# Attention scores on 64x128 tiles, with the scale moved from the turned queries into the maximum pass

## Chip, core and metric

The kernel runs on one core of one Trainium2 chip. The metric is the device time of one execution in microseconds. In the profile the engines are PE (TensorE matmul), PEld (its weight loads), DVE (VectorE), ACT (ScalarE), POOL (GpSimd) and SP (SyncE, whose queue issues nearly all DMAs).

## What is computed

```python
def _attn_ref(q, k, v, tau):            # 8 batches, 8 heads, 576 rows, 64 columns
    scale = 1.0 / np.sqrt(q.shape[-1])
    scores = scale * np.matmul(q, k.transpose(0, 1, 3, 2))
    thresh = np.max(scores, axis=-1, keepdims=True) - tau
    scores = np.where(scores >= thresh, scores, -1000000000.0)
    scores = scores - np.max(scores, axis=-1, keepdims=True)
    attn = np.exp(scores)
    attn = attn / (np.sum(attn, axis=-1, keepdims=True) + 1e-09)
    return np.matmul(attn, v)

def _moe_ref(x, w_in, w_out):           # 4608x512, 512x2048, 2048x512
    h = np.maximum(x @ w_in, 0.0)
    return h * h @ w_out
```

The attention output, with its heads side by side, is `x`. All of it is float32; the two weight matrices arrive as float64 and are converted on the core.

## The kernel before

**Stages.** First comes attention, in 72 periods (`period`, L631). Periods 2 to 34 also convert the weights (`CONVERTING`, the names c1 to c6: L208, L214, L221, L229, L237, L248); periods 35 to 71 don't (`PLAIN`), and POOL adds up weight blocks there. Then come the two dense layers, done as sums and products of blocks (L946 and L1085 on PE, L125 and L128 on DVE and POOL). The change touches attention alone.

**Units.** Two heads of a batch are a pair; there are 32 pairs. The 576 query rows of a pair are four blocks of 128 and a rest of 64. A *unit* is one block of one pair, for both of its heads (j = 0, 1); the rests of two pairs form one unit together. So two pairs give 4 + 4 + 1 units, 144 in all, 16 of them shared by two pairs. A period computes the scores and the softmax of two units, called A and B, and the value products of the two units of two periods before.

**The steps of a period.** The lists `PLAIN` and `CONVERTING` (L606 and L609) write out the order by hand; each engine runs its part of a list in this order.

- *T*, `turn` (L399): PE transposes rows of q or of k, 64 rows at a time (L406), on tiles of 64 rows by 128 columns, into two banks of PSUM. *eT* copies the result to SBUF. For q that is two scaled copies of 256 columns on ACT (L413, an activation with `scale=qscale`, a column of 128 values, each -1/8). For k it is two plain copies (L421, 256 and 320 columns), and a scaled one (L413, 64 columns) for the query rest, whose rows are turned along with the keys. Every pair has a turn of q and a turn of k, so nine periods have four of each, and one has none.
- *SA*, *SB*, `scores` (L434): products of queries and keys. The contraction is over 64 values (one head), so the PE array is used in tiles. Before, all are tiles of 64x64: per unit two heads times two halves of 64 query rows, each a matmul of 512 columns (the first eight 64-key blocks) and one of 64 (the rest). SA does the 512 columns of A, and then the 64 of A and of B; SB does the 512 of B. A float32 matmul shows as two records.
- *topA0* and so on, `top` (L463): for each unit and head DVE reads 576 columns of scores from PSUM, multiplies them by a constant 1.0, writes them to SBUF, and takes the minimum (the scale is negative, so the minimum stands for the maximum). The accumulator is read by a second record. These four are "the passes" below. PLAIN has them as A1, A0, B1, B0.
- *least* (L470, POOL) adds tau to the minimum. *pow* (L473, ACT) is the exponential. *mask* (L478, DVE) sets what is below the threshold to zero, and sums; its threshold is a column of 128 values.
- *over*, *inv* (L485 POOL, L488 DVE): the reciprocals of the sums. *spread* (L528, POOL) widens them to 64 columns each.
- *U*, *V*, *W* (`half_turn`, L388): PE transposes the weights, also on 64x128 tiles; W also turns the widened reciprocals. *eU*, *eV*, *eW* (L535) are the copies on ACT.
- *PV*, `values` (L544): products of values and turned weights, on 64x64 tiles, into banks 0 and 5.
- *x* (L658 to L671): the two heads' products leave PSUM. Head 0's is multiplied by the reciprocals on DVE as it is read (L665, 128 columns); head 1's is copied by ACT (L667). *xs* (L682): POOL multiplies head 1's copy by its reciprocals. Then DMAs store x.

**What shares banks.** Scores, turned rows, the turn W and value products share six banks of PSUM. Unit A's scores lie in banks 0, 1, 4 and 5, unit B's in 1 to 4, the value products in 0 and 5, turned rows in 1 and 4, W in 2 and 3. `touch` (L363) adds a wait wherever two engines meet in a bank: PV waits for the passes over A, SA waits for the copies of x, the rest columns wait for eT, SB waits for eW. U and V use two further banks and wait for each other's copies.

In PLAIN the order on PE is SA, SB, V, PV, T, W, U; in CONVERTING it is T, SA, U, SB, PV, V, W.

## Time and profile before

| | |
|---|---|
| Median of three runs | 1281.25 us (1281.09 to 1282.95) |
| Span of the profiled execution, first to last instruction | 1278.6 us |
| Median less that span | 2.65 us |
| First pass (L463) of the first and of the last period | 9.5 us and 479.5 us |
| PE busy over the span | 1255.2 us (98%) |
| DVE, ACT, POOL busy over the span | 1000.2, 855.6, 897.4 us (78%, 67%, 70%) |
| Granted TensorE clock | 1.000 |

The shares over the whole span mix attention, in which PE, DVE and ACT are all busy nearly throughout, with the dense layers, in which PE alone is. What bounds attention has to be read from its own stages. A timeline row has the start (us from the span's start), the time until the last of its records ends, the engine, the line, the operation, the tiles written and read, the shape, the count, and in brackets the idle time before it with what ended that. Records on ACT and PE overlap: the next one can start before the last has ended, so what one of them costs is the distance between starts. A windows row has, for each engine, its busy time and its records in brackets.

### The profile page before, as it was taken

What the parts mean: (1) busy time and instruction counts of PE and PEld (TensorE: products, weight loads), DVE (VectorE), ACT (ScalarE), POOL (GpSimd) and SP (SyncE); (2) the same over time, 40 slices, a digit from 0 to 9 for tenths busy, and PEclk for the clock granted to TensorE, in tenths of its full rate; (3) what the DMA queues carried; (4) which work ended last, traced back from release to release, by engine and by line L of the source; (5) the groups of instructions that cost most, each with busy time, mean ns of one, the idle gap of its engine ahead of it and who ended that gap; (6) DMA issues with size and microseconds to landing.
All of it is one profiled execution on the core that took longest, in us unless ns stands there. A gap on an engine that the chain in (4) does not pass through costs nothing.

```text
span 1278.6 us, 44201 instructions
## 1 busy us (share of the span) xinstructions
PE 1255.2 (98%) x17459; PEld 1087.0 (85%) x17459; DVE 1000.2 (78%) x2449; ACT 855.6 (67%) x1552; POOL 897.4 (70%) x1094
## 2 busy tenths in 40 slices
PE   8999999999999999999999999999999999999998
PEld 6666666677777768988888888999999999999998
DVE  6999999999999997787878877877645664565463
ACT  6999999999999995666765767667422441343240
POOL 2565665655555557888798889858877777786775
PEclk9999999999999999999999999999999999999999
DMA  6566666544333413457666666589635414522511
GB/s 155 152 158 160 165 193 182 151 94 112 89 83 84 97 34 98 156 164 219 198 190 204 192 198 187 177 324 394 208 122 166 133 50 149 166 95 76 161 35 34
DMA packets 256591, 191.89 MB, mean 150 GB/s; under 512 B 96000, under 2 KB 217344, under 8 KB 256384
## 3 DMA queue, kind: packets, MB, share of 16 engines
q1 hardware_dynamic: 254928, 188.63, 49.8%
q8 instruction: 137, 2.24, 0.7%
q14 instruction: 70, 0.57, 0.1%
q10 hardware_dynamic: 1456, 0.44, 0.1%
HBM read 116.65 MB, written 72.35 MB: 148 GB/s over the span
## 4 chain that ended last, share of the span: by engine, by line
PE 70%; DMA 1%; ACT 1%; DVE 1%; issue 1%; ACTq 0%; DVEq 0%; SPq 0%
PE po L1085 30%; PE ph L946 27%; PE sc L544 5%; PE sc L445 4%; PE pt L388 2%; DMA wall<-w 1%; PE sc L406 1%; PE sc L388 1%; DVE arena L128 1%; DVE arena L463 0%; DMA g<-arena 0%; ACT arena L916 0%; ACT c L879 0%; DMA arena<-xT 0%; ACT arena L917 0%
## 5 line engine op out<-in xcount | busy, mean ns | idle before, releaser
L128 POOL TENSOR_TENSOR arena<-arena 128x512 f32<-128x512 f32 (+1 forms) x314 | 377.7, 1222 | 126.3 <-DVE arena L128 89.4
L1085 PE MATMUL po<-wall,arena 128*128 128x128 f32 x3528 | 394.4, 275 | 0.2 <-DVE arena L125 0.2
L1085 PEld LDWEIGHTS po<-wall,arena 128*128 128x128 f32 x3528 | 394.1, 192 | 0.4 <-DVE arena L125 0.4
L946 PE MATMUL ph<-arena,wall 128*128 128x128 f32 (+1 forms) x2352 | 387.4, 327 | 1.1 <-DVE arena L665 0.5
L946 PEld LDWEIGHTS ph<-arena,wall 128*128 128x128 f32 x2352 | 354.2, 191 | 34.2 <-DVE arena L128 2.2
L128 DVE TENSOR_TENSOR arena<-ph,arena 128x512 f32<-128x512 f32 x378 | 255.6, 688 | 75.8 <-PE ph L946 50.0
L125 POOL TENSOR_TENSOR arena<-arena 128x128 f32<-128x128 f32 (+2 forms) x314 | 255.2, 814 | 29.1 <-DMA arena<-w 10.7
L879 ACT COPY c<-arena 128x512 f32<-128x512 f32 (+2 forms) x319 | 176.1, 558 | 104.2 <-DVE arena L125 85.7
L473 ACT ACTIVATE arena<-arena 128x576 f32<-128x576 f32 x288 | 232.1, 918 | 16.7 <-DVE arena L463 16.7
L128 DVE TENSOR_TENSOR arena<-po,arena 128x128 f32<-128x128 f32 x378 | 108.3, 290 | 168.0 <-PE po L1085 167.4
L478 DVE SCALAR_TENSOR_TENSOR arena<-arena 128x576 f32<-128x576 f32 x288 | 225.5, 811 | 0.4 <-POOL arena L470 0.4
L463 DVE TENSOR_SCALAR_CACHE_REDUCE arena<-sc 128x576 f32<-128x576 f32 x288 | 204.5, 751 | 14.3 <-ACT arena L535 6.4
L125 DVE TENSOR_TENSOR arena<-arena,c 128x512 f32<-128x512 f32 (+2 forms) x283 | 176.8, 633 | 7.9 <-ACT c L879 6.1
L544 PEld LDWEIGHTS sc<-arena 64*64 64x64 f32 x5760 | 144.4, 133 | 43.1 <-DVE arena L463 39.1
L445 PE MATMUL sc<-arena 64*64 64x64 f32 (+1 forms) x2304 | 170.0, 415 | 0.3 <-DVE arena L665 0.3
L544 PE MATMUL sc<-arena 64*64 64x128 f32 (+1 forms) x5760 | 160.8, 262 | 8.5 <-DVE arena L463 5.8
L535 ACT COPY arena<-pt 128x1024 f32<-128x1024 f32 x144 | 166.0, 1153 | 1.6 <-PE pt L388 1.5
L769 ACT COPY arena<-po 128x128 f32<-128x128 f32 x63 | 16.6, 264 | 185.4 <-PE po L1085 185.4
L388 PEld LDWEIGHTS pt<-ident,arena 64*128 64x128 f32 x2304 | 83.0, 138 | 41.7 <-ACT arena L535 33.8
L388 PE MATMUL pt<-ident,arena 64*128 64x64 f32 x2304 | 100.8, 227 | 2.4 <-ACT arena L535 2.1
L445 PEld LDWEIGHTS sc<-arena 64*64 64x64 f32 x2304 | 62.5, 132 | 47.5 <-issue 22.7
L470 POOL TENSOR_SCALAR arena<-arena,tau_p 128x2 f32<-128x2 f32 x144 | 65.5, 455 | 41.8 <-DVE arena L463 35.2
(51 smaller groups left out, 936.6 us busy)
## 6 DMA issues: line engine op xcount, KB each, us to landing
g<-arena SPq DMA_DIRECT2D x144, 256.0 KB, 2.6
arena<-g SPq DMA_DIRECT2D x144, 256.0 KB, 4.5
w<-arena SPq DMA_DIRECT2D x60, 256.0 KB, 2.8
wall<-w SPq DMA_DIRECT2D x49, 256.0 KB, 5.3
arena<-w SPq DMA_DIRECT2D x44, 256.0 KB, 3.1
arena<-in_v_dram SPq DMA_DIRECT2D x32, 288.0 KB, 4.6
out_dram<-arena SPq DMA_DIRECT2D x70, 128.0 KB, 2.4
arena<-in_q_dram SPq DMA_DIRECT2D x64, 128.0 KB, 4.1
```

Source lines behind the costliest of these rows:

```text
L125: e.tensor_tensor(out=out, in0=x, in1=y, op=ALU.subtract)
L128: e.tensor_tensor(out=out, in0=x, in1=y, op=ALU.add)
L388: made = nc.tensor.transpose(pt[:, r, ts(slot, HALF)], of[rows, :], ident[rows, rows])
L445: made = nc.tensor.matmul(sc[at, ds(to, count)], lhs, kT[rows, ds(at_k, count)], start=True, stop=True)
L463: made = nc.vector.tensor_scalar(out=s[:, j, :], in0=sc[:, ds(at, S)], scalar1=1.0, scalar2=None, op0=ALU.mult, op1=ALU.min, accum_out=nmx ...
L473: nc.scalar.activation(out=w[:, :, j, :], in_=of(j), func=AF.Exp, bias=nmx[:, j : j + 1], scale=-1.0)
L478: nc.vector.scalar_tensor_tensor(out=w[:, :, j, :], in0=of(j), scalar=thr[:, j : j + 1], in1=w[:, :, j, :], op0=ALU.is_le, op1=ALU.mult, a ...
L535: touch("weights", nc.scalar.copy(joined(to), whole(pt, 0, count)), at, 2 * BANK, m)
L544: made = nc.tensor.matmul(sc[ds(u * D, D), ds(5 * j * BANK + row, count)], loaded_v[i][rows, (c - (u != j)) % CH, :], wT[m][rows, ds(weigh ...
L879: nc.scalar.copy(c, y)
L946: nc.tensor.matmul(to[:, j, :], W_IN[m, k][:, ts(h * parts_ + j, P)], x_of(m, k), start=(not more and j == 0), stop=True, skip_group_check ...
L1085: nc.tensor.matmul(to, g[:, j, :], w[:, j, :], start=(not more and j == 0), stop=(j == 3), skip_group_check=True)
```

## The change

Four edits, all in attention:

1. **Scores of units of one pair** go on 64x128 tiles: one matmul per head with all 128 query rows and not two with 64. The turned queries are stored so that a unit's 128 rows lie side by side, and the turned keys as two halves of 320 columns (256 of keys, and 64 which hold the query rest in half 0 and the key rest in half 1). Units that two pairs share keep two matmuls per head on 64x64 tiles.
2. **The scale** is applied in the maximum pass: its constant 1.0 becomes the column `qscale`.
3. **Turned rows** are copied plain, in two copies of 256 columns for q and two of 320 for k. The separate copy of the query rest is gone.
4. **Value products** are copied plain by ACT for both heads, and POOL multiplies both at once (256 columns).

```diff
             turned[i] = (
                 sb.tile([P, MAIN], FP32, tag="qT", bufs=Q_RING, name="qT"),
-                sb.tile([P, S], FP32, tag="kT", bufs=K_RING, name="kT"),
-                sb.tile([P, REST], FP32, tag="qR", bufs=K_RING, name="qR"),
+                sb.tile([P, 2, (FULL + 1) * HALF], FP32, tag="kT", bufs=K_RING, name="kT"),
             )
...
         def then():
-            part = lambda r, x, n: (spots[r][0][:, ds(x, n)], spots[r][1])
+            for r, copy_by in enumerate((nc.scalar.copy, other or nc.scalar.copy)):
+                part, half = spots[r][0][:, 0:n], to[which][:, r, :] if which else joined(to[0])[:, r, :, :]
+                part = part if which else part.rearrange("p (t q) -> p t q", q=HALF)
+                touch(kind, copy_by(half, part), spots[r][1], BANK, i)
             if which:
-                for r, n in ((0, half), (1, half + REST)):
-                    spot = part(r, 0, n)
-                    copy_by = other if r and other else nc.scalar.copy
-                    touch(kind, copy_by(to[1][:, ds(r * half, n)], spot[0]), spot[1], BANK, i)
-                scaled(to[2], part(0, half, REST))
                 next_keys(i)
             else:
-                for r in range(2):
-                    scaled(to[0][:, ds(r * half, half)], part(r, 0, half))
...
-            for c in range(2):
-                rows, at = ds(j * D, D), ds(c * HALF, HALF)
-                qT, kT, qR = turned[of[c]]
-                lhs = qT[rows, ds((c * FULL + t) * HALF, HALF)] if t < FULL else qR[rows, :]
-                made = nc.tensor.matmul(
-                    sc[at, ds(to, count)], lhs, kT[rows, ds(at_k, count)], start=True, stop=True
-                )
-                touch("q scores" if t < FULL else "scores", made, to, count, of[c])
+            rows = ds(j * D, D)
+            if t < FULL:
+                lhs_of = [(slice(0, P), of[0], turned[of[0]][0][rows, ts(t, P)])]
+            else:
+                lhs_of = [(ds(c * HALF, HALF), of[c], turned[of[c]][1][rows, 0, ds(FULL * HALF, REST)]) for c in range(2)]
+            for at, i, lhs in lhs_of:
+                kT = turned[i][1]
+                keys = kT[rows, 1, ds(FULL * HALF, REST)] if rest else kT[rows, :, 0 : FULL * HALF]
+                to_ = sc[at, ds(to, count)] if rest else sc[at, ds(to, count)].rearrange("p (r n) -> p r n", r=2)
+                made = nc.tensor.matmul(to_, lhs, keys, start=True, stop=True)
+                touch("q scores" if t < FULL else "scores", made, to, count, i)
...
-                out=s[:, j, :], in0=sc[:, ds(at, S)], scalar1=1.0, scalar2=None,
+                out=s[:, j, :], in0=sc[:, ds(at, S)], scalar1=qscale[:, :], scalar2=None,
...
-                by_vector = (0,)
                 for j in range(2):
-                    by = sc[:, ds(5 * j * BANK, P)], wT[m][:, ts(SCALE_AT + j, P)]
-                    if j in by_vector:
-                        made = nc.vector.tensor_tensor(out=x[:, j, :], in0=by[0], in1=by[1], op=ALU.mult)
-                    else:
-                        made = nc.scalar.copy(x[:, j, :], by[0])
-                    touch("x", made, 5 * j * BANK, P, m)
+                    touch("x", nc.scalar.copy(x[:, j, :], sc[:, ds(5 * j * BANK, P)]), 5 * j * BANK, P, m)
...
+                flat = x[:, :, :].rearrange("p j q -> p (j q)")
+                nc.gpsimd.tensor_tensor(out=flat, in0=flat, in1=by, op=ALU.mult)
```

More of the change, by code (lines that the diff above doesn't have):

```diff
@@ L407, in turn @@
                 touch("turns", made, at, BANK)
-        half = FULL * HALF
-        kind = "turned k" if which else "turned q"
-        def scaled(to, spot):
-            touch(kind, nc.scalar.activation(out=to, in_=spot[0], func=AF.Identity, scale=qscale[:, :]), spot[1], BANK, i)
+        kind, n = "turned k" if which else "turned q", (FULL + (1 if which else 0)) * HALF
         def then():
-            part = lambda r, x, n: (spots[r][0][:, ds(x, n)], spots[r][1])
+            for r, copy_by in enumerate((nc.scalar.copy, other or nc.scalar.copy)):
+                part, half = spots[r][0][:, 0:n], to[which][:, r, :] if which else joined(to[0])[:, r, :, :]
+                part = part if which else part.rearrange("p (t q) -> p t q", q=HALF)
+                touch(kind, copy_by(half, part), spots[r][1], BANK, i)
             if which:
-                for r, n in ((0, half), (1, half + REST)):
-                    spot = part(r, 0, n)
-                    copy_by = other if r and other else nc.scalar.copy
-                    touch(kind, copy_by(to[1][:, ds(r * half, n)], spot[0]), spot[1], BANK, i)
-                scaled(to[2], part(0, half, REST))
                 next_keys(i)
             else:
-                for r in range(2):
-                    scaled(to[0][:, ds(r * half, half)], part(r, 0, half))
-                for n in later_loads(i, 0):
-                    load_q(n)
+                for n_ in later_loads(i, 0):
+                    load_q(n_)
         return then
@@ L436, in scores @@
         of, t = units[n]
-        at_k, count = (MAIN, REST) if rest else (0, MAIN)
+        count = REST if rest else MAIN
         for j in range(2):
```

11 lines of the change are left out of this document (2 added, 9 removed).

## The prediction, made before the changed kernel had run

> **What bounds the kernel now.** The span comes first, then the shares of the engines in two stretches, then the timelines of single periods inside them. A period is the work on two units; the kernel has 72 of them, then the two dense layers, which the change doesn't touch.
>
> ```profile
> span 1278.6 us, 44201 instructions
> ```
>
> The runs have a median of 1281.25 us, 2.65 us more than this span; I keep that difference and sum against the span. The windows by engine, and the same windows for the vector engine's maximum pass alone (its count is eight records a period: four passes, each with a read of the accumulator):
>
> ```profile
> 49.54:238.83 189.29, 180.58 (x4340) 126.45 (x4340) 187.39 (x541) 189.29 (x333) 114.41 (x190) 1.00 0.66 173
> 259.87:467.40 207.53, 206.13 (x5270) 149.32 (x5266) 199.19 (x594) 198.60 (x338) 114.50 (x198) 1.00 0.37 86
> ```
>
> ```profile
> 49.54:238.83 189.29, 77.18 (x216) 1.00 0.66 173
> 259.87:467.40 207.53, 94.27 (x264) 1.00 0.37 86
> ```
>
> The columns are length, PE, PEld, DVE, ACT, POOL. So 216/8 = 27 periods of 7.01 us in the first window and 264/8 = 33 of 6.29 us in the second. They are two stages with two limits. In **stage C** (weights are converted as well; 33 periods) ACT is busy for all 189.29 us and DVE for 187.39, 6.94 a period: ACT sets the pace, with DVE 0.07 behind it. In **stage P** (37 periods) PE is busy for 206.13 of 207.53, and ACT and DVE each idle for over 0.25 us a period. There a loop through two engines sets the pace:
>
> ```profile
> 389.45 0.52 PE L406 MATMUL sc<-ident,arena 64*128 64x64 f32 x10
> 389.81 0.41 PE L388 MATMUL sc<-ident,arena 64*128 64x64 f32 x8
> 390.06 0.66 PE L388 MATMUL pt<-ident,arena 64*128 64x64 f32 x16
> 390.65 2.33 PE L445 MATMUL sc<-arena 64*64 64x512 f32 x32
> 392.91 0.72 PE L388 MATMUL pt<-ident,arena 64*128 64x64 f32 x16
> 393.62 0.45 PE L544 MATMUL sc<-arena 64*64 64x128 f32 x8
> ```
>
> ```profile
> 392.12 0.76 DVE L463 TENSOR_SCALAR_CACHE_REDUCE arena<-sc 128x576 f32<-128x576 f32 x1 [0.27 <-ACT arena L535]
> ...
> 392.80 0.75 DVE L463 TENSOR_SCALAR_CACHE_REDUCE arena<-sc 128x576 f32<-128x576 f32 x1
> ```
>
> Scores start at 390.65; the first pass at 392.12, once the first unit's scores and the 64-column rest are there; the second ends at 392.80 + 0.75 = 393.55; the value products, which overwrite the banks that these two read, start 0.07 later; then come the turns and the next scores. What shortens the step from the last turn to the first pass, or lengthens the first two passes, moves the period one for one. The other two passes, the masks and the exponentials have the idle time above as cover.
>
> **The change part by part.**
>
> *ACT: plain copies of turned rows, and both value copies.* Stage C:
>
> ```profile
> 158.51 1.24 ACT L413 ACTIVATE arena<-sc,qscale 128x256 f32<-128x256 f32 x2
> 159.23 0.68 ACT L667 COPY arena<-sc 128x128 f32<-128x128 f32 x1
> 159.37 1.21 ACT L473 ACTIVATE arena<-arena 128x576 f32<-128x576 f32 x1
> ...
> 165.49 1.14 ACT L421 COPY arena<-sc 128x256 f32<-128x256 f32 x2
> 166.06 0.78 ACT L413 ACTIVATE arena<-sc,qscale 128x64 f32<-128x64 f32 x1
> 166.27 0.72 ACT L667 COPY arena<-sc 128x128 f32<-128x128 f32 x1
> ```
>
> Durations overlap here, so I go from start to start. Two scaled q halves of 256 columns take 159.23 - 158.51 = 0.72; two plain k copies (256 and 320) take 0.57, so 512 plain columns take about 0.51 and 640 about 0.63. The scaled 64 columns take 0.21, a value copy 0.14. A period that turns q changes by 0.51 - 0.72 + 0.14 = -0.07, one that turns k by 0.63 - 0.78 + 0.14 = -0.01, one without a turn by +0.14. Of nine periods four turn q, four k, one nothing: -0.02 on average, over 33 periods **-0.7 us**. In stage P this is covered by ACT's idle time.
>
> *DVE: the scale is read from a column.* The pass had the constant 1.0 and gets `qscale`, one value per partition in SBUF; a DVE pass over PSUM with such an operand isn't in the trace. The nearest rows:
>
> ```profile
> L128 DVE TENSOR_TENSOR arena<-ph,arena 128x512 f32<-128x512 f32 x378 | 255.6, 688 | 75.8 <-PE ph L946 50.0
> ...
> L478 DVE SCALAR_TENSOR_TENSOR arena<-arena 128x576 f32<-128x576 f32 x288 | 225.5, 811 | 0.4 <-POOL arena L470 0.4
> L463 DVE TENSOR_SCALAR_CACHE_REDUCE arena<-sc 128x576 f32<-128x576 f32 x288 | 204.5, 751 | 14.3 <-ACT arena L535 6.4
> ```
>
> The mask has the same 576 columns and the same accumulator, and takes 811 against 751 ns. It has a second source and a column operand more. The second source seems free: L128 has two, and with 64 columns fewer is 63 ns shorter than the pass. So 0.06 us is left for the column. The lower end is 0 (the second source may be the reason after all); the upper is ACT's price, (0.72 - 0.51)/2 = 0.105. I take **0.06**, four times a period.
>
> *DVE loses a product.* From 158.86 to 159.06 in stage C:
>
> ```profile
> 158.86 0.28 DVE L665 TENSOR_TENSOR arena<-sc,arena 128x128 f32<-128x128 f32 x1
> ...
> 159.06 0.81 DVE L478 SCALAR_TENSOR_TENSOR arena<-arena 128x576 f32<-128x576 f32 x1
> ```
>
> That is -0.20 against 4 x 0.06 = +0.24: DVE in stage C goes from 6.94 to 6.98, still under ACT's 6.99. Nothing is won or lost there, and the cover is 0.01 us. In stage P the product isn't in the loop, but two of the four passes are: +0.12 a period.
>
> *PE: half the score instructions, and one tile shape with the turns.* The columns that stream stay the same: four 64x64 tiles side by side become two 64x128 tiles side by side. What changes is the seam. Turns run in pairs: eight pairs take 0.66 (from 390.06), four take 0.41 (from 389.81), so pairs start 0.25/4 = 0.063 apart, a record is 0.22 long, and the last of the eight starts at 390.06 + 7 x 0.063 = 390.50. The scores start at 390.65, not at 390.56: 0.09 lost, and the first weights (up to 0.06, a turn's spacing) are loaded in the open. With the turns' shape kept I take 0.13 off this seam; bounds 0 and 0.15. The seam from scores to turns (392.91) has the same gain, but the value products after it wait for the second pass, so it moves nothing.
>
> In the Trainium skill, "TensorEngine Tiling (Array Packing)", Key Properties, a change of tiling mode drains the array, and a change of tile within a mode doesn't. By it the whole 0.15 goes; the trace can't tell a change of shape from a change from transposes to products, since at every seam here both change.
>
> Could something else hold the scores then? They need the value products copied out, now both by ACT, and behind them on PE wait the rest columns, the turns and the second unit's scores:
>
> ```profile
> 389.61 0.27 ACT L667 COPY arena<-sc 128x128 f32<-128x128 f32 x1
> 389.78 0.78 ACT L473 ACTIVATE arena<-arena 128x576 f32<-128x576 f32 x1
> 390.45 0.69 ACT L421 COPY arena<-sc 128x256 f32<-128x256 f32 x2
> 391.02 0.34 ACT L413 ACTIVATE arena<-sc,qscale 128x64 f32<-128x64 f32 x1
> ```
>
> The second copy would end near 389.78 + 0.27 = 390.05, before 390.56. The rest columns overwrite the banks of the turned rows, whose last read ends at 391.36; afterwards it is 0.17 later by the value copy and 0.15 earlier by the turned copies, about the same. That holds the rest a few hundredths in a k period, which is why I take 0.13 and not 0.15.
>
> *Units shared by two pairs* keep 64x64 tiles: 16 of 144, nine of them in stage P. As first unit of a period (4) the old seam stays and a new one comes before the second unit's rest: +0.09. As second unit (5) the seam moves into the rest: -0.13 + 0.09 = -0.04.
>
> *POOL* multiplies 256 columns in one go and not 128:
>
> ```profile
> L682 POOL TENSOR_TENSOR arena<-arena 128x128 f32<-128x128 f32 x72 | 35.9, 499 | 20.5 <-ACT arena L667 19.8 <-DMA arena<-in_k_dram 0.8
> ```
>
> Behind it wait the small sums and their reciprocals, and on SP's queue the store of the result and loads for a later period. POOL idles for 2.8 us a period in both windows, which hides it; without that cover it would be up to 0.5 a period.
>
> *The start.* The fillers before the first scores wait for the scaled 64 columns:
>
> ```profile
> 7.53 0.42 PEld L1137 LDWEIGHTS sc<-ident 128*128 128x128 f32 x4 [0.82 <-ACT arena L413]
> ```
>
> That copy goes and the one before it grows by 64 columns: **-0.2 us**. At the end of the stage the second copy (0.14) and part of POOL's longer product come once in the open: +0.2.
>
> **The sum.** Stage P: 28 plain periods x (-0.13 + 0.12) = -0.3; 4 x (0.09 + 0.12) = +0.8; 5 x (-0.04 + 0.12) = +0.4: together **+0.9**. With -0.7, -0.2 and +0.2 this is +0.2 on 1278.6 and as much on the median: **1281.5 us**, no difference. Its own range, 1279 to 1284, is the seam at 0.10 to 0.15 and the column at 0.04 to 0.07.
>
> **The rivals.**
>
> *The column costs DVE nothing.* Then the loop is 0.12 shorter in each of 37 periods, -4.4 us, and ACT keeps stage C where it is: **1277 us**. For it: the mask's 60 ns could be its second source. Against: L128.
>
> *The seam stays* (the change doesn't do what it says on PE): going from transposes to products costs the gap even in one shape. The 0.13 is lost in 33 periods, +4.3: **1286 us**. For it: every turn-to-score seam in the trace has this gap. Against: nothing in the trace, only the rule above.
>
> *The column costs what it costs ACT, 0.105* — the case on the slower side. Then DVE in stage C needs 6.94 - 0.20 + 0.42 = 7.16 and takes over from ACT's 6.99: 33 x 0.17 = +5.6; in stage P 37 x 2 x 0.045 = +3.3: **1290 us**. It decides from about 0.065 on, where DVE passes ACT. For it: the margin is only 0.01 us. Against: the mask's whole excess is 0.06.
>
> *Weights of the second half of a product wait for the first.* With four tiles the loads overlap the stream:
>
> ```profile
> 390.65 0.21 PEld L445 LDWEIGHTS sc<-arena 64*64 64x64 f32 x8
> ```
>
> Eight loads are through in 0.21 us, while the scores run 2.33. If two wide tiles can't do this, three more loads stand in the open in each loop, up to a turn pair's 0.06 each: 37 x 0.18 = +6.7, **1288 us**. Against: the turns, on the same wide tiles, come every 0.063 with a load each. The Trainium skill, "TensorE: Matmul & The Clock Gate", The mechanism, has loads overlap running products only in other row groups; the row above speaks against it.
>
> **How the numbers follow.** Forecast 0.53, free column 0.17, seam stays 0.13, dear column 0.08, loads in the open 0.05, and 0.04 for a gain that I don't see. A measurement of this kernel can tell about 0.2%, 2.6 us, from no change. The forecast's own range lies inside that, the rivals outside: faster 0.21, same 0.53, slower 0.26. The range goes from the free column to the loads in the open, 1276.5 to 1288, and leaves out the dear column and the tails, under 2 in 10.
>
> **What would show it.** The pass's mean duration: 811 ns for the forecast, 751 for the free column, over 850 for the dear one. The seam: scores 0.06 after the start of the last turn pair, and not 0.15. Stage C: ACT busy throughout, periods of 7.0 us. Stage P: 6.29 us a period within 0.03. The forecast is wrong if stage C leaves 7.0 by more than 0.05 a period, or if the first pass in stage P is held by something else than PE's rest columns.

## The result, and the profile after

The changed kernel takes **1292.22 us** (median of 4 runs, 1292.14 to 1292.9); the kernel before, run beside it, 1281.17 (1280.67 to 1282.95, 4 runs). The ratio is 1.0084, with a 95% interval of 1.007 to 1.0098: 11 us slower. The forecast was 1281.5, its range ended at 1288, so the time lies outside, on the slow side.

The page of the changed kernel, and the first pass of its last period, from its timeline:

```profile
span 1290.4 us, 42204 instructions
```

```profile
491.47 0.81 DVE L456 TENSOR_SCALAR_CACHE_REDUCE arena<-sc,qscale 128x576 f32<-128x576 f32 x1
```

Before, that pass started at 479.5. So 12.0 us were lost in attention, and the span is 11.8 longer: the dense layers took the same time within 0.2. In this kernel the passes are L456, the masks L471, scores L440, turns L405, half turns L387, value products L537, both value copies L655, POOL's product L664 and spread L521.

**By stage.** The next rows are windows cut from the first pass of one period to the first pass of another. The first holds 31 converting periods, the second 34 plain ones; the columns are length, PE, PEld, DVE, ACT, POOL. First before, then after:

```profile
22.27:238.83 216.56, 206.51 (x4942) 144.47 (x4942) 214.45 (x619) 216.51 (x381) 128.44 (x214) 1.00 0.64 168
259.87:473.47 213.60, 212.14 (x5450) 153.64 (x5446) 205.26 (x612) 203.89 (x346) 117.93 (x204) 1.00 0.37 86
```

```profile
23.01:241.59 218.58, 196.69 (x4494) 148.81 (x4492) 218.09 (x588) 217.56 (x398) 137.00 (x214) 1.00 0.62 164
263.18:485.02 221.84, 209.84 (x4960) 164.00 (x4958) 221.07 (x579) 206.88 (x365) 128.55 (x204) 1.00 0.36 83
```

A converting period went from 216.56/31 = 6.99 to 7.05, a plain one from 213.60/34 = 6.28 to 6.52. That makes 2.0 and 8.2 us; the other 1.8 are in the start and the first two periods, the three where the stages meet, and the last. The column to look at is DVE: before, it was idle for 8 us of the plain window, now it is busy for 221.07 of 221.84, though it lost 33 instructions there (612 to 579).

**DVE's groups** say where that time is:

```profile
L471 DVE SCALAR_TENSOR_TENSOR arena<-arena 128x576 f32<-128x576 f32 x288 | 242.0, 885 | 0.3 <-POOL arena L463 0.3
L456 DVE TENSOR_SCALAR_CACHE_REDUCE arena<-sc,qscale 128x576 f32<-128x576 f32 x288 | 219.8, 807 | 5.3 <-PE sc L440 3.2 <-PE sc L405 1.1 <-ACT arena L208 0.4
```

The pass takes 807 ns and not 751: the column costs 56 ns a record, as forecast. But the mask, which the change does not touch, went from 811 to 885. Its single records in a plain and in a converting period, with POOL's beside them:

```profile
404.23 0.82 DVE L471 SCALAR_TENSOR_TENSOR arena<-arena 128x576 f32<-128x576 f32 x1
404.89 0.74 POOL L664 TENSOR_TENSOR arena<-arena 128x256 f32<-128x256 f32 x1 [0.43 <-ACT arena L655]
...
404.97 1.28 DVE L471 SCALAR_TENSOR_TENSOR arena<-arena 128x576 f32<-128x576 f32 x1
...
406.18 0.81 DVE L471 SCALAR_TENSOR_TENSOR arena<-arena 128x576 f32<-128x576 f32 x1
```

```profile
152.96 0.42 DVE L229 TENSOR_SCALAR arena<-arena 128x512 int32<-128x512 int32 x1
...
153.38 0.79 DVE L471 SCALAR_TENSOR_TENSOR arena<-arena 128x576 f32<-128x576 f32 x1
153.60 0.83 POOL L521 COPY arena<-arena 128x256 f32<-128x256 f32 x1
...
154.10 0.94 DVE L471 SCALAR_TENSOR_TENSOR arena<-arena 128x576 f32<-128x576 f32 x1
```

The third mask of the plain period takes 1.28 instead of 0.81. It starts 0.08 after POOL's 256-wide product. The second mask of the converting period takes 0.94, and it starts while POOL's spread runs. There is no idle time ahead of either mask, so no view of waits shows this: the wait is inside the instruction. Both masks end 0.61 to 0.62 after POOL's instruction does (405.63 and 406.25, 154.43 and 155.04). So does the held mask, the third or the fourth, in each of the 34 plain periods of the window. Before, the spread ran as long:

```profile
158.36 0.83 POOL L528 COPY arena<-arena 128x256 f32<-128x256 f32 x1
```

But then DVE's product ran behind the first mask (158.86 in the prediction's rows), and the second mask kept its 0.81. The mask reads two tiles in SBUF, the scores and their exponentials. In the Trainium skill, "SBUF — State Buffer", Who interferes with whom, a DVE instruction with two SBUF inputs contends with a GpSimd instruction that reads SBUF; whichever starts first holds the other off until it is done. The trace agrees: 0.47 and 0.13 us.

**PE's loop.** The steps that the prediction took from 390.06, 390.65 and 392.12, now:

```profile
398.33 0.66 PE L387 MATMUL pt<-ident,arena 64*128 64x64 f32 x16
398.83 2.48 PE L440 MATMUL sc<-arena 64*128 64x512 f32 x16
```

```profile
400.47 0.82 DVE L456 TENSOR_SCALAR_CACHE_REDUCE arena<-sc,qscale 128x576 f32<-128x576 f32 x1
```

From the start of the turns to the scores it is 0.50, not 0.59: the seam gave 0.09. But from the scores to the first pass it is 1.64, not 1.47, in this period with a turn of k. The 0.17 is in the rest products. One more loop of before, from its timeline, and then windows of PE's score records of 64 columns, before and after (four and two of the records counted are the last of 512 columns, still streaming):

```profile
403.17 2.33 PE L445 MATMUL sc<-arena 64*64 64x512 f32 x32
```

```profile
404.07:404.28 0.21, 0.21 (x20) 1.00 0.05 10
```

```profile
399.74:400.09 0.35, 0.35 (x10) 1.00 0.04 8
```

Sixteen records on 64x64 tiles took 0.21, eight on 64x128 tiles take 0.35; both begin 0.9 after the scores (404.07 - 403.17, 399.74 - 398.83). The first pass follows the end of these windows by nearly the same time in both, 0.36 before (it starts at 404.64) and 0.38 after (400.47). The groups of the weight loads by form, of the scores and of the half turns:

```profile
L440 PEld LDWEIGHTS sc<-arena 64*128 64x128 f32 x1024 | 81.9, 188 | 28.2 <-issue 16.4 <-ACT arena L413 7.7
L387 PEld LDWEIGHTS sc<-ident,arena 64*128 64x128 f32 x576 | 25.8, 138 | 3.2 <-issue 1.4 <-POOL arena L521 0.4 <-DVE arena L456 0.3
...
L440 PEld LDWEIGHTS sc<-arena 64*64 64x64 f32 x256 | 7.5, 132 | 5.2 <-issue 2.2 <-ACT arena L413 1.1
```

A load of the same 64x128 tile takes 188 ns for a product and 138 for a half turn. That is where the prediction went astray: it held the spacing of turns against this rival. Whether the load is also what sets the slower pace stays open (see the tiles below).

### The profile page after: what moved, and what is told of

Same layout as the page of the kernel before. It is cut to its first block, busy times and chain, and to the rows that moved or that the text cites. A ratio compares the mean times of both kernels' runs of the same rounds, so it can differ in the third digit from the quotient of the medians.

```text
span 1290.4 us, 42204 instructions
## 1 busy us (share of the span) xinstructions
PE 1243.3 (96%) x16435; PEld 1103.7 (86%) x16435; DVE 1021.8 (79%) x2377; ACT 860.0 (67%) x1592; POOL 918.2 (71%) x1094
## 4 chain that ended last, share of the span: by engine, by line
PE 61%; ACT 1%; DVE 1%; issue 0%; DMA 0%; ACTq 0%; DVEq 0%
PE po L1067 30%; PE ph L928 29%; PE sc L537 1%; PE sc L440 1%; DVE arena L456 0%; ACT c L861 0%; DMA wall<-w 0%; ACT arena L898 0%; DVE arena L128 0%; PE pt L387 0%; PE sc L387 0%; DVE arena L125 0%; ACT arena L899 0%; ACT arena L528 0%; ACT arena L751 0%
## 5 line engine op out<-in xcount | busy, mean ns | idle before, releaser
L471 DVE SCALAR_TENSOR_TENSOR arena<-arena 128x576 f32<-128x576 f32 x288 | 242.0, 885 | 0.3 <-POOL arena L463 0.3
L466 ACT ACTIVATE arena<-arena 128x576 f32<-128x576 f32 x288 | 223.2, 832 | 23.1 <-DVE arena L456 23.1
L456 DVE TENSOR_SCALAR_CACHE_REDUCE arena<-sc,qscale 128x576 f32<-128x576 f32 x288 | 219.8, 807 | 5.3 <-PE sc L440 3.2
L537 PEld LDWEIGHTS sc<-arena 64*64 64x64 f32 x5760 | 144.4, 133 | 68.7 <-DVE arena L456 68.2
L537 PE MATMUL sc<-arena 64*64 64x128 f32 (+1 forms) x5760 | 160.5, 262 | 35.9 <-DVE arena L456 35.6
L440 PE MATMUL sc<-arena 64*128 64x512 f32 (+3 forms) x1280 | 181.0, 437 | 0.0
L528 ACT COPY arena<-pt 128x1024 f32<-128x1024 f32 x144 | 153.7, 1068 | 1.8 <-PE pt L387 1.6
L440 PEld LDWEIGHTS sc<-arena 64*128 64x128 f32 (+1 forms) x1280 | 89.4, 177 | 33.4 <-issue 18.6
L387 PEld LDWEIGHTS pt<-ident,arena 64*128 64x128 f32 x2304 | 85.0, 139 | 31.2 <-ACT arena L528 23.5
L387 PE MATMUL pt<-ident,arena 64*128 64x64 f32 x2304 | 98.4, 225 | 1.5 <-ACT arena L528 1.2
L899 ACT ACTIVATE arena<-arena 128x512 f32<-128x512 f32 x144 | 90.8, 630 | 4.6
```

The source lines that it names most:

```text
L387: made = nc.tensor.transpose(pt[:, r, ts(slot, HALF)], of[rows, :], ident[rows, rows])
L440: made = nc.tensor.matmul(to_, lhs, keys, start=True, stop=True)
L456: made = nc.vector.tensor_scalar(out=s[:, j, :], in0=sc[:, ds(at, S)], scalar1=qscale[:, :], scalar2=None, op0=ALU.mult, op1=ALU.min, accu ...
L466: nc.scalar.activation(out=w[:, :, j, :], in_=of(j), func=AF.Exp, bias=nmx[:, j : j + 1], scale=-1.0)
L471: nc.vector.scalar_tensor_tensor(out=w[:, :, j, :], in0=of(j), scalar=thr[:, j : j + 1], in1=w[:, :, j, :], op0=ALU.is_le, op1=ALU.mult, a ...
L528: touch("weights", nc.scalar.copy(joined(to), whole(pt, 0, count)), at, 2 * BANK, m)
```

## The experiments

The theory after this reading had three parts: **(1)** the column costs 0.06 in every pass, and in the converting stage nothing hides it; **(2)** on wide tiles the short rest products wait for their weights, which eats the seam's gain; **(3)** POOL's product and spread hold DVE's masks, because DVE's product no longer stands between them. The main rivals: the column is hidden in the converting stage; the tiles gain; the mask is stretched by something else than POOL.

All kernels are in one table. The periods are the lengths of windows cut as above, divided by 31 and by 34. The kernel before ran beside each group of experiments, and its medians differ by up to 0.5 us:

| Kernel | Median, us | Ratio, 95% | Converting | Plain |
|---|---|---|---|---|
| Before | 1280.78 to 1281.32 | | 6.99 | 6.28 |
| Changed | 1292.22 | 1.007 to 1.0098 | 7.05 | 6.52 |
| Column alone | 1291.81 | 1.0072 to 1.0104 | 7.14 | 6.39 |
| Changed, constant in the pass | 1284.98 | 1.0012 to 1.0042 | 6.97 | 6.42 |
| Wide tiles alone | 1284.26 | 1.0015 to 1.0034 | 6.99 | 6.38 |
| Wide tiles, narrow rest | 1283.55 | 1.0008 to 1.0028 | 6.96 | 6.37 |
| Edit 4 alone | 1291.92 | 1.0071 to 1.0101 | 7.13 | 6.48 |
| Changed, edit 4 undone | 1294.06 | 1.0085 to 1.0119 | 7.10 | 6.52 |
| Changed, POOL's product later | 1290.33 | 1.006 to 1.009 | 7.07 | 6.45 |
| Changed, narrow tiles | 1291.43 | 1.0073 to 1.0101 | 7.09 | 6.52 |
| Changed, narrow and later | 1287.36 | 1.0037 to 1.0062 | 7.06 | 6.37 |
| Changed, early spread | 1292.45 | 1.0076 to 1.0104 | 7.04 | 6.54 |
| Changed, spread clear | 1294.4 | 1.0091 to 1.0121 | 7.11 | 6.53 |
| Changed, three stalls out | 1289.69 | 1.0056 to 1.009 | 7.13 | 6.38 |
| Plain copies and wide tiles | 1280.74 | 0.9991 to 1.0009 | 6.87 | 6.38 |
| Plain copies, narrow tiles | 1280.07 | 0.9981 to 0.9999 | 6.92 | 6.30 |

### The column

*Column alone*, on the kernel before:

```diff
+    ones = const.tile([P, 1], FP32, name="ones")
+    nc.gpsimd.memset(ones[:, :], 1.0)
...
-                out=s[:, j, :], in0=sc[:, ds(at, S)], scalar1=1.0, scalar2=None,
+                out=s[:, j, :], in0=sc[:, ds(at, S)], scalar1=ones[:, :], scalar2=None,
```

> The kernel before with edit 2's cost alone: the pass reads its factor 1.0 from a column of ones. Theory: 0.06 us in each of four passes. Plain periods 6.28 + 2 x 0.06 = 6.40; converting ones no longer hide it behind ACT, because DVE's floor there is 6.87 and not 6.94, and with four passes becomes 7.11 against a mean of 6.99 before: 33 x 0.12 + 37 x 0.12 = 8.4, time 1289 to 1290. Rival (the blind forecast: ACT's 6.99 covers most of it in the converting stage): 1285 to 1287.

Measured: 1291.81 us (1289.68 to 1295.58, 5 runs), as much as the whole change. The pass is L465 here; the group and the windows:

```profile
L465 DVE TENSOR_SCALAR_CACHE_REDUCE arena<-sc,ones 128x576 f32<-128x576 f32 x288 | 220.2, 811 | 9.5 <-PE sc L447 3.7 <-issue 1.7 <-PE sc L408 1.1
```

```profile
24.20:245.64 221.44, 199.87 (x4952) 142.78 (x4956) 219.94 (x617) 217.56 (x380) 127.22 (x213) 1.00 0.58 162
267.04:484.28 217.24, 212.01 (x5450) 153.42 (x5446) 212.77 (x612) 205.86 (x346) 120.94 (x204) 1.00 0.34 85
```

A pass takes 811 ns, a plain period 6.39 and a converting one 7.14, with DVE busy for 219.94 of 221.44. The theory's periods hold, and the rival's cover by ACT is not there. The time is over the 1290 expected; in the profiled execution two single periods are about 1.1 us longer than their neighbours.

*The constant in the changed kernel*, which leaves out what the column gives for a negative tau:

```diff
-                out=s[:, j, :], in0=sc[:, ds(at, S)], scalar1=qscale[:, :], scalar2=None,
+                out=s[:, j, :], in0=sc[:, ds(at, S)], scalar1=-SCALE, scalar2=None,
```

> The changed kernel with the constant -1/8 in the maximum pass in place of the column (this leaves out what the column gives for a negative tau). Theory (column 0.06 us in each of four passes, wherever DVE or the loop through the first two passes sets the pace): pass record 807 to about 750 ns, converting periods from 7.05 to about 6.96 (ACT's bound), plain ones from 6.53 by 0.12 to 0.24, to 6.29 to 6.41. Time 1282 to 1286. Rival (the passes have cover, and the loss is all POOL's and PE's): 1291 to 1292.

1284.98 us (1284.52 to 1285.65), 7.2 under the changed kernel, as theory (1) has it. The converting period is back at 6.97, where the prediction had ACT's bound (6.99 less 0.02). What is left, 4 us, is parts (2) and (3). Part (1) by itself would make the kernel as slow as it is, and without it the other edits still lose: the costs don't add.

### The tiles

*Wide tiles alone*, on the kernel before: edit 1 and the new layout, with the scaled copies, the constant 1.0 and DVE's product as before.

```diff
-            for c in range(2):
-                rows, at = ds(j * D, D), ds(c * HALF, HALF)
...
+                lhs_of = [(slice(0, P), of[0], turned[of[0]][0][rows, ts(t, P)])]
```

> The kernel before with edit 1 alone (scores of units of one pair on 64x128 tiles, new layout); the scaled copies, the constant 1.0 in the pass and DVE's product stay. Theory: the seam from the last turn to the scores shrinks by 0.09 (starts 0.06 apart and not 0.15), but the rest products, 64 columns long, now come in pairs every 0.11 (loads of 128 weight columns, which so short a stream does not cover), and the way from the first score to the first pass grows from 1.47 to about 1.63. The two nearly cancel: plain periods 6.29 before, 6.31 to 6.36 here, converting ones 7.0; time 1281 to 1284. Rival 1 (the seam is all there is): plain periods 6.16, time 1276. Rival 2 (the wide tiles are the bulk of the change's loss): plain periods 6.45 and more, over 1287.

1284.26 us (10 runs), ratio 1.0024, 0.3 over the end of what was expected: a small loss where the prediction had a gain of some 3.5 us. The passes are L467, the scores L451; windows of the stages, one loop, and the rest:

```profile
22.63:239.21 216.58, 203.13 (x4498) 150.73 (x4496) 214.06 (x619) 215.93 (x381) 128.44 (x214) 1.00 0.62 167
260.25:477.17 216.92, 210.51 (x4960) 161.56 (x4960) 205.43 (x612) 203.95 (x346) 117.82 (x204) 1.00 0.36 84
```

```profile
405.01 0.66 PE L387 MATMUL pt<-ident,arena 64*128 64x64 f32 x16
405.51 2.46 PE L451 MATMUL sc<-arena 64*128 64x512 f32 x16
```

```profile
407.16 0.76 DVE L467 TENSOR_SCALAR_CACHE_REDUCE arena<-sc 128x576 f32<-128x576 f32 x1 [0.36 <-ACT arena L539]
```

From the turns to the scores it is 0.50 (0.59 before), and from the scores to the pass 1.65 (1.47 before): -0.09 and +0.18. Plain periods are 0.10 longer on average. That mean hides five kinds, as the starts of the first passes show: a period with a turn of q is 0.04 longer (its scores to pass take 1.60) and one with a turn of k 0.08. One without a turn is mostly 0.18 longer, for there the seam gave nothing. With a shared unit it is 0.23 longer where that unit comes first, and 0.15 where it comes second. The prediction had -0.13 for the first three kinds, and +0.09 and -0.04 for the shared units. The converting stage is untouched, since its bound is elsewhere. Both rivals fall.

*The same with the rest on narrow tiles:*

```diff
+                if rest:
+                    lhs_of = [(ds(c * HALF, HALF), of[0], turned[of[0]][0][rows, ds(t * P + c * HALF, HALF)]) for c in range(2)]
```

> As the kernel with edit 1 alone, but only the products of 512 columns are on 64x128 tiles; the rest products of 64 columns stay on 64x64 tiles. Theory (long loads that short streams do not cover): the four products of a rest come every 0.06 again; a change of tile shape of 0.09 now stands between the 512 columns and the rest; first score to first pass 1.50 to 1.57 where all-wide has 1.63; plain periods 6.22 to 6.28, time 1278 to 1281. Rival (the rest takes longer for another reason, such as the new layout of the keys): 1.63 and the time of the all-wide kernel.

1283.55 us (9 runs): no better, and outside the 1278 to 1281 expected. The time is the rival's, but not for the rival's reason. Its windows of the first scores and of the rest, and one loop (passes L469, scores L453):

```profile
405.78:406.28 0.50, 0.49 (x4) 1.00 0.00 0
406.79:407.04 0.25, 0.25 (x18) 1.00 0.14 29
```

```profile
405.79 2.53 PE L453 MATMUL sc<-arena 64*128 64x512 f32 x24
```

```profile
407.40 0.76 DVE L469 TENSOR_SCALAR_CACHE_REDUCE arena<-sc 128x576 f32<-128x576 f32 x1 [0.33 <-ACT arena L541]
```

The sixteen records of the rest are quick again, 0.25 against 0.35, so for products the tile's width set their pace, and the new layout of the keys did not. But the rest starts 406.79 - 405.79 = 1.00 after the scores, where it was 0.90 before (404.07 - 403.17): the change of tile shape now stands inside the scores, and 0.10 is lost there. Scores to pass is 1.61. The seam can be moved within this loop; neither layout removes it for less than it costs. Whether the load itself or another step of a wide product sets the 0.11 per pair of records was not tried.

### POOL's product and DVE's mask

*Edit 4 alone*, on the kernel before:

```diff
-                by_vector = (0,)
+                by_vector = ()
```

> The kernel before with edit 4 alone: both value products copied plain by ACT, POOL multiplies 256 columns. Theory: the third mask of a plain period is stretched by 0.4 to 0.5 us here too, but DVE has about 0.25 us a period to spare, so plain periods grow by 0 to 0.2 (6.29 to at most 6.45); converting periods are ACT's and grow by the extra copy less what there is of slack, about 0.08 to 0.14. Time 1284 to 1290. Rival (POOL's product costs nothing without the other edits): only ACT's copy in 33 converting periods, 1284, and the mask at 0.8.

1291.92 us (1290.87 to 1292.8, 4 runs), above the range. Three rows: POOL's product with a mask, and one wait of POOL.

```profile
407.57 1.33 POOL L677 TENSOR_TENSOR arena<-arena 128x256 f32<-128x256 f32 x1 [0.58 <-ACT arena L667]
...
408.24 1.28 DVE L478 SCALAR_TENSOR_TENSOR arena<-arena 128x576 f32<-128x576 f32 x1
```

```profile
327.61 1.26 POOL L125 TENSOR_TENSOR arena<-arena 128x512 f32<-128x512 f32 x1 [4.88 <-DMA arena<-xT]
```

Here POOL's product starts under the third mask, takes 1.33 instead of 0.74, and holds the fourth mask to 1.28: each holds the other in turn. In the converting stage the second mask takes 0.94 here too, which puts that stretch down to edit 4; but DVE has room there, and the stage pays one copy on ACT, 0.14 a period, the price that the prediction gave it. In the plain stage a single wait for one load (4.88 us; 1.52 at the same block before) makes one period 3.8 us longer. Without it a plain period is 6.37, 0.09 over before, and the time of this execution, the slowest of the four at 1292.8, would be about 1289. Why that load landed late stays open.

*Edit 4 undone in the changed kernel:*

```diff
+                by_vector = (0,)
...
-                    touch("x", nc.scalar.copy(x[:, j, :], sc[:, ds(5 * j * BANK, P)]), 5 * j * BANK, P, m)
...
+                    if j in by_vector:
+                        made = nc.vector.tensor_tensor(out=x[:, j, :], in0=by[0], in1=by[1], op=ALU.mult)
+                    else:
+                        made = nc.scalar.copy(x[:, j, :], by[0])
...
```

> The changed kernel with edit 4 undone: DVE multiplies head 0's value products as it reads them, POOL multiplies 128 columns. Theory (POOL's 256-wide product holds DVE's third mask, 0.47 us in each plain period, and POOL's spread holds the second mask in converting periods): the third mask of a plain period goes from 1.28 back to at most 0.85 us, plain periods are then set by PE's loop, 6.48 with a turn of k and 6.41 with a turn of q, against 6.53 on average; the converting ones keep 7.0 to 7.1. Time 1289.5 to 1291, about 2 under the changed kernel. Rival 1 (the mask is stretched by something else, for instance the column operand of the passes): the mask stays at 1.28 and the time at 1292. Rival 2 (POOL's product is the whole loss): back to 1282.

1294.06 us (1292.72 to 1295.23): no gain, where about 2 us were expected, though the masks are freed, as the group shows (816 ns on average, 885 in the changed kernel).

```profile
L471 DVE SCALAR_TENSOR_TENSOR arena<-arena 128x576 f32<-128x576 f32 x288 | 226.2, 816 | 0.2 <-POOL arena L463 0.2
```

```profile
23.46:243.43 219.97, 194.49 (x4494) 146.99 (x4492) 219.97 (x619) 214.04 (x366) 127.59 (x214) 1.00 0.60 163
265.01:486.67 221.66, 209.80 (x4960) 166.65 (x4958) 213.12 (x612) 200.91 (x331) 120.95 (x205) 1.00 0.35 83
```

My expectation left out that DVE gets its 0.20 back: in the converting stage it is now busy for every microsecond (219.97 of 219.97), at 7.10. In the plain stage DVE has 8 us idle again, and the period stays 6.52. In most periods with a turn PE's loop is the bound, at 6.49 to 6.59, as in the changed kernel (6.48 to 6.59). Without a turn the period is 6.41, because the scores now wait for DVE's product: they start 0.06 after it ends.

*POOL's product at another moment.* In plain periods it, and with it the store of x, comes after the small sums of the next period; no instruction is added or taken away:

```diff
-        fetch U SA topA1 over s1 topA0 SB topB1 inv ...
+        fetch U SA topA1 over xl s1 topA0 SB topB1 inv ...
...
+        steps["xl"] = lambda: pending and pending.pop()()
```

> The changed kernel with the same instructions, but in plain periods POOL's 256-wide product comes after the small sums of the next period, when DVE is at passes over PSUM, and not between the third and the fourth mask. Theory (the product holds a mask because both read two SBUF sources at the same moment): third mask from 1.28 to 0.74 to 0.85 us, plain periods 6.48 (k), 6.41 (q), 6.17 (no turn), time about 1289.5, as with the edit undone. Rival (POOL's width itself, or another thing that edit 4 did, sets it): mask and time unchanged, 1292; if the later product holds up the reciprocals instead, slower than 1292.

1290.33 us (1290.28 to 1291.01), plain periods 6.45. POOL's product (L668 here) now meets a pass, whose scores come from PSUM:

```profile
406.38 0.73 POOL L668 TENSOR_TENSOR arena<-arena 128x256 f32<-128x256 f32 x1
406.51 0.82 DVE L456 TENSOR_SCALAR_CACHE_REDUCE arena<-sc,qscale 128x576 f32<-128x576 f32 x1 [0.53 <-ACT arena L528]
```

Neither is stretched, and the mask's mean falls to 824 ns. Only the moment differs, so the meeting was the cause of the 1.28. It was worth 1.9 us of the 11. Period by period, those with a turn change by at most 0.06 (most take 6.48 to 6.59 in both kernels), though a mask was held in each: PE's loop covered it. Most of the gain is in the five without a turn, four of which go from 6.45 to 6.06; one wait for a load (0.45) is not met here.

### Two bounds side by side

*The changed kernel with scores on 64x64 tiles* (the edit below), and *the same with POOL's product later* (the edit above as well):

```diff
-                lhs_of = [(slice(0, P), of[0], turned[of[0]][0][rows, ts(t, P)])]
+                lhs_of = [(ds(c * HALF, HALF), of[0], turned[of[0]][0][rows, ds(t * P + c * HALF, HALF)]) for c in range(2)]
```

> The changed kernel with all scores back on 64x64 tiles. Theory (two bounds lie side by side in the plain stage: PE's loop, which this shortens to 6.40, and DVE with the stretched mask at 6.45 to 6.48, which stays): plain periods 6.44 to 6.48, where the changed kernel has 6.53; converting ones unchanged at 7.05; time 1289.5 to 1291. Rival (the costs simply add): plain periods shorter by the 0.10 that the wide tiles cost alone, 1288.5.

> The changed kernel with scores on 64x64 tiles and, in plain periods, POOL's product after the small sums of the next period: both bounds of the plain stage taken away. Theory: plain periods 6.40 with a turn, 6.1 without, as the kernel before plus 0.12 for the column in two passes, mean 6.38 to 6.40; converting ones unchanged at 7.05; time 1286.5 to 1288.5, more below the changed kernel (4 to 5.5) than either step by itself gives. Rival (another bound stands at 6.45): 1290.

1291.43 us (1291.11 to 1294.17) and 1287.36 us (1286.57 to 1287.77). The plain stage of each:

```profile
265.30:487.04 221.74, 212.50 (x5454) 155.44 (x5446) 219.94 (x579) 206.77 (x365) 128.04 (x204) 1.00 0.36 83
```

```profile
263.68:480.13 216.45, 211.92 (x5450) 155.55 (x5446) 205.92 (x578) 206.50 (x365) 122.65 (x205) 1.00 0.36 84
```

With narrow tiles alone DVE is the bound (219.94 of 221.74). One period again waits for a load and is 1.9 us longer; without it the mean is 6.47, as expected, and the time is 0.4 over what was expected. With both steps the time is as expected. Taking away one of the two, tiles or mask, gains 0.8 and 1.9 us; both together gain 4.9. What remains over before in the plain stage, 6.37 against 6.28, is the column in two passes.

### The converting stage

*The spread earlier*, beside a pass; and *earlier still*, ahead of unit A's threshold, so that it also clears the conversion on DVE (L229):

```diff
-        ... c3 topA0 U eU powA1 SB topB0 over topB1 powA0 c4 powB0 PV eT inv leastA maskA1 x powB1 leastB spread ...
+        ... over c3 topA0 U eU powA1 SB topB0 inv leastA spread topB1 powA0 c4 powB0 PV eT maskA1 x powB1 leastB ...
```

```diff
-        ... SB topB0 inv leastA spread topB1 ...
+        ... SB topB0 inv spread leastA topB1 ...
```

> The changed kernel; in converting periods alone POOL's small sums, DVE's reciprocal and POOL's spread come earlier, so that the spread runs beside a pass over PSUM and not beside a mask. Theory (the spread stretches the second mask of a converting period by 0.13, since the product on DVE that used to stand between them is gone): second mask from 0.94 to 0.81, DVE's floor from 7.05 to 6.91, converting periods 6.92 to 6.96 (ACT's bound), time 1288 to 1290. Rival (the mask is stretched by something else, or ACT holds the stage at 7.05 too): mask or period unchanged, 1292.

> As the kernel with the early spread, but POOL's spread also ahead of unit A's threshold, so that it begins some 0.24 us earlier and should end before DVE's weight-conversion instruction (which there was stretched from 0.42 to 0.54 in place of the mask). Theory (DVE's floor holds the converting stage and the spread adds 0.12 to 0.13 to it wherever it meets a DVE instruction that works from SBUF alone): neither the mask (0.81) nor the conversion (0.42) is stretched, converting periods 6.91 to 6.97, time about 3 us under the changed kernel, 1288.5 to 1290. Rival (ACT or PE holds the stage at 7.04): both short and the period still 7.04, 1292.

1292.45 us (1291.75 to 1293.08) and 1294.4 us (1294.11 to 1294.85): both outside what was expected. The first:

```profile
152.97 0.39 POOL L521 COPY arena<-arena 128x256 f32<-128x256 f32 x1
...
153.10 0.54 DVE L229 TENSOR_SCALAR arena<-arena 128x512 int32<-128x512 int32 x1
...
154.31 0.81 DVE L471 SCALAR_TENSOR_TENSOR arena<-arena 128x576 f32<-128x576 f32 x1
```

The second mask is 0.81 again, but the conversion went from 0.42 to 0.54: the spread now holds that one. In the second kernel:

```profile
154.18 0.79 POOL L463 TENSOR_SCALAR arena<-arena,tau_p 128x2 f32<-128x2 f32 x2
...
154.21 0.42 DVE L229 TENSOR_SCALAR arena<-arena 128x512 int32<-128x512 int32 x1
154.74 0.82 DVE L471 SCALAR_TENSOR_TENSOR arena<-arena 128x576 f32<-128x576 f32 x1
```

Now the conversion is short and the mask is short, but POOL's threshold of unit A comes behind the spread, and the mask waits for it: it starts at 154.74, and the conversion ended at 154.21 + 0.42 = 154.63. From the conversion's start to the mask's is 0.53, where the conversion alone takes 0.34 (from 152.96 to DVE's next instruction, at 153.30, in the changed kernel): 0.19 is lost. The period follows DVE's delay each time (7.04, 7.11), which speaks against ACT or PE holding the stage at 7.04. That it would fall to 6.91 without any delay was not reached, and is only worked out.

*Narrow tiles, product later and this spread together:*

> The changed kernel without the three stalls that are not the column's: scores on 64x64 tiles, POOL's product at a pass over PSUM in plain periods, POOL's spread at a pass in converting ones. Theory: plain periods 6.37 as with the first two, converting ones 6.91 to 6.97; time 1283.5 to 1286, and what is left over the kernel before, 3 to 5 us, is the column in two passes of the 37 plain periods. Rival (the converting stage does not move): 1287.4.

1289.69 us (1288.63 to 1291.31), over the 1286 expected. The plain periods are as expected (6.38); the converting ones are worse (7.13), for the reason just given.

### Versions that leave the column and edit 4 out

*The constant -1/8 with edit 4 undone* (a negative tau is left out): plain copies of turned rows on wide, and on narrow tiles. The edits are those shown above.

> The changed kernel with the constant -1/8 in the pass (this leaves out a negative tau) and edit 4 undone: what is left of the change is the wide tiles and the plain copies of turned rows. Theory: the third mask is 0.81 again, converting periods go to DVE's 6.94 or just under (ACT has 0.15 less to do), plain ones to PE's loop of 6.31 to 6.36; time 1279 to 1282. Rival (ACT still sets the converting stage): 7.0 there, 1282 to 1284.

> As the kernel before, with the plain copies of turned rows in the new layout and the constant -1/8 in the pass (this leaves out a negative tau); scores on 64x64 tiles, DVE's product as before. Theory: plain periods as before, 6.29; converting ones from 6.99 to DVE's 6.94 or a little less, since ACT loses 0.15 in periods with a turn; time 1278 to 1280.5, one to three under the kernel before. Rival (the plain copies change nothing, since DVE was the bound of the converting stage all along): 1281.

1280.74 us (1279.26 to 1283.44, 11 runs) and 1280.07 us (1277.57 to 1281.68, 11 runs). Both times are as expected; the plain periods of the first, 6.38, are just over. The rows are the converting stage of the first, and both stages of the second:

```profile
22.13:235.21 213.08, 192.53 (x4495) 145.13 (x4494) 212.61 (x619) 212.07 (x367) 128.01 (x214) 1.00 0.62 169
```

```profile
22.75:237.32 214.57, 196.94 (x4942) 140.50 (x4942) 213.04 (x619) 212.51 (x367) 128.57 (x214) 1.00 0.63 170
258.46:472.76 214.30, 208.45 (x5450) 151.87 (x5446) 205.29 (x612) 198.86 (x331) 117.85 (x204) 1.00 0.36 86
```

213.08/31 = 6.87 with DVE busy for 212.61: that is DVE's floor in the converting stage when ACT is relieved. The narrow version is 0.1% under the kernel before (ratio 0.9981 to 0.9999), which can hardly be told from nothing.

## Why the prediction was wrong

- **"With the turns' shape kept I take 0.13 off this seam"**. This is the step that failed most. The seam gave 0.09 (0.06 from the last turn pair to the scores, the sign that the prediction had named), and the rest products on wide tiles cost 0.13 to 0.18 in the same loop, for which the sum had no term. The tiles were entered at 28 x (-0.13) + 4 x 0.09 + 5 x (-0.04) = -3.5 us; alone they cost +2.9 (1284.26 against 1281.32). Two thirds of what the plain window lost (216.92 against 213.60) come from periods with a shared unit or without a turn, where the sum's +0.09, -0.04 and -0.13 were +0.23, +0.15 and up to +0.18. The mechanism had been named as a rival, loads in the open at 0.18 a period, and given 0.05, because turns on the same tiles come every 0.063. The load of a turn is not that of a product: 138 against 188 ns.
- **"DVE in stage C goes from 6.94 to 6.98, still under ACT's 6.99. Nothing is won or lost there, and the cover is 0.01 us."** Wrong by its cover. DVE's 6.94 had been read where ACT set the pace; its floor, read where it is the bound, is 6.87. Taken from that the sum is 6.87 - 0.20 + 0.24 = 6.91; to it came 0.13 that was not in the sum, because the product that went had stood between the first mask and the second while the spread ran (158.86 and 159.06 in the prediction's row). That makes 7.04; measured 7.05. That the forecast's 6.98 is only 0.07 off is luck: a floor 0.07 too high stood against a stretch of 0.13 left out. The stage came out 2.0 us slower over 31 periods, where -0.7 was forecast. DVE took the stage over, as the rival "dear column" had it, but not because the column costs more than 0.06.
- **"POOL idles for 2.8 us a period in both windows, which hides it"**. It hid POOL's time, not DVE's: the product held a mask for 0.47 in each plain period. Most of that lies behind PE's longer loop; moving it gained 1.9 us, most of it in periods without a turn.
- **What held.** The column's price: 0.06 forecast, 0.056 and 0.060 by the records. The rival of a free column and that of a seam that stays are refuted. ACT's savings are real, but worth something only where ACT is the bound: in the changed kernel DVE is.

Together: 6.4 us for the tiles, 2.7 for the converting stage and 1.9 for the mask make 11.0, against the 10.7 between 1281.5 and 1292.22. The three overlap, as the pairs of experiments show, so this is an account of sizes and not a sum of independent parts.

## What to carry to other kernels

An instruction that goes may have kept two others apart: before it is taken away or made wider, look at which DVE instructions work from SBUF alone and what POOL does beside them, and look for the damage in mean durations, since no wait is shown. Price an operand, a load or a cover from a row of the same kind: a product's weights from products and not from turns, and an engine's floor from a stage in which it alone is the bound. Where two bounds lie 0.1 us apart, undoing one part tells little; undo them in pairs.

## What the runs showed of the hardware

- A DVE pass over 576 columns of PSUM whose factor is a column and not a constant takes 0.06 us longer (751 to 807 and 811 ns).
- DVE and POOL hold each other off for whole instructions, with no idle time shown: a held mask ends 0.61 to 0.62 after POOL's instruction. A mask went from 0.81 to 1.28 and 0.94, a one-source conversion of 512 columns from 0.42 to 0.54, POOL's product from 0.74 to 1.33. Beside a pass that reads PSUM, neither was stretched (0.82 and 0.73). The conversion has one SBUF source only. In the Trainium skill, "SBUF — State Buffer", Who interferes with whom, such an instruction contends when it runs in a mode that uses both ports; the 0.54 agrees with that, and nothing else here shows the mode.
- Pairs of float32 products of 64 columns on 64x128 tiles came about every 0.11 us, four at a time on 64x64 tiles about every 0.06: eight records in 0.35, sixteen in 0.21. Turns on 64x128 tiles came every 0.063. Which step of a wide product takes the longer time is not shown.
